# First 256 rows of k and q of batch 0 loaded in float32 by SyncE's queue, with the ALiBi table made in two parts

## The chip, the cores and the metric

The kernel runs on one core of a Trainium2 chip. The metric is the device time of one execution in microseconds (us), as the median over runs. The engines are TensorE (PE; its weight loads are PEld), VectorE (DVE), ScalarE (ACT), GpSimd (POOL) and SyncE (SP). DMAs are issued by an engine into its queue: POOL's is q0 in the profile, SP's is q1, and both are carried out by the core's 16 DMA engines.

## The reference

Sliding-window attention with ALiBi, then a feed-forward layer with ELU. All inputs and the output are float32.

```python
# q, k, v: (8, 8, 576, 64) = batch, heads, sequence, head size
scores = q @ k.T / 8 + slope[h] * -(abs(i - j))      # slope[h] = 2 ** -(h + 1)
scores = where((i >= j) & (i - j < 128), scores, -1e9)
attn = exp(scores - max) / (sum + 1e-9)
x = (attn @ v).transpose(0, 2, 1, 3).reshape(4608, 512)
h = x @ w_in                                          # (512, 2048)
out = where(h > 0, h, exp(min(h, 0)) - 1) @ w_out     # (2048, 512)
```

## The kernel before

Work is in float16 on TensorE with float32 sums in PSUM. Each batch of 576 rows goes through attention, is turned into columns of `xT`, and then feeds the two products of the feed-forward layer: `hidden` (L297, `x @ w_in`, matmuls at L305), `elu` (L319, DVE at L323) and `output` or the seven products of a Strassen scheme (L393). An order written out by hand interleaves these: steps ("slots") numbered from 0, with lists `early`, `HID`, `tasks`, `OUT` and `late` for each (L491 to L668). `at(s, f, ...)` puts a call into slot s. Each engine executes its instructions in the order in which they are written, and POOL also issues every load, in the order written, with at most eight loads of its queue unfinished at a time.

The change touches the opening, L428 to L488, which is ahead of slot 0. It goes through these stages:

- DVE fills `wz` with ones (L430) and TensorE runs 22 matmuls on it (`warm`, L465) that compute nothing that is used.
- POOL issues loads with `load_first` (L98), `load_v` (L112) and `load_wi` (L117), which round float32 to float16 on the way. First come rows 0 to 255 of k of batch 0 (L431), then the `iota` that the masks are made of (L432), the same rows of q (L433), two blocks of v (L434, L435), a quarter of `w_in` (L436), and the remaining rows of q and k. `split` (L90) says how the rows lie: rows 0 to 255 lie on 64 partitions with four rows each.
- DVE makes the identity, the bias row `RB` and `SI`, the identity scaled by each head's slope (L454 to L461). ScalarE makes the table `TAB[:, 0]` of exp(bias) for eight heads (L464).
- `turn_first` (L127) transposes q and k on TensorE into a PSUM bank and copies the bank into `K0` or `Q0`. It is called for each half of k (L466, L467; both copied by DVE) and of q (L469 by ScalarE, L470 by DVE). `early_bias` (L179) adds the bias to a bank by matmuls with `SI`.
- DVE copies `RB` (L471, L472) and `TAB` (L473, L474) into the shape of a batch's last unit. Batch 0 doesn't read `TAB`; batch 1 is the first that does (L216).
- `early_scores` (L186), `early_expo` (L194, ScalarE's exp) and `values` (L243, the product with v, then a division on DVE at L259 and L260) give the first 256 rows of attention. `turn` (L280) transposes them into `xT`, and the first `hidden` of slot 0 starts.

Slots 3 and 4 matter too. In slot 3 DVE's list holds `elu` of slot 2 (L323). In slot 4 it holds `values(0, 2, ...)`, that is a reciprocal (L259) and a product (L260) for each half, and then `elu` of slot 3. In slot 5 comes the copy of `turn(0, 2)` (L290).

`st` is a pair of buffers that hold q and k of batches 2 to 7 as loaded; the changed kernel borrows one of them once. `fore[2]` is a buffer that is first written in slot 13.

Of the kernel before, what the change touches and what calls it, by code (L numbers as in the profile page):

```python
# [7 lines left out]
F32 = mybir.dt.float32  # L8
F16 = mybir.dt.float16
I32 = mybir.dt.int32  # L10
AF = mybir.ActivationFunctionType
# [7 lines left out]
def kernel(  # L19
# [9 lines left out]
    nc = tc.nc  # L29
    B, H, S, D = q.shape  # L30
# [6 lines left out]
    R = S // 64  # L37
    V = nc.vector

    const = ctx.enter_context(tc.tile_pool(name="const", bufs=1))  # L40
    stage = ctx.enter_context(tc.tile_pool(name="stage", bufs=2))
# [7 lines left out]
    def one(shape, dt, name):  # L49
        return const.tile(shape, dt, name=name, tag=name)  # L50
# [6 lines left out]
    fore = [t.rearrange("p j c -> p (j c)") if t is not None else None for t in T]  # L57
    RB = fore[3][:, 1024:1536]
# [3 lines left out]
    TAB = one([128, 2, 4, 2, 256], F16, "TAB")  # L62
# [22 lines left out]
    st = {}  # L85
    s0 = gpool.tile([128, NFC * 512], F16, name="s0", tag="g")
    s1 = one([128, 2 * H * 6 * D], F16, "s1")
    s0 = [t[:, 0:2 * H * 6 * D].rearrange("p (w h j d) -> p w h j d", w=2, h=H, j=6) for t in (s0, s1)]

    def split(b, w, part):  # L90

        if b == 0 and w == 1:
            return ((0, 64, 4, 0, 0), (64, 64, 5, 256, 0))[part]
        if b == 0:
            return ((0, 64, 4, 0, 0), (64, 64, 2, 256, 0), (64, 64, 3, 384, 2))[part]
        return ((0, 128, 4, 0, 0), (0, 64, 1, 512, 4))[part]

    def load_first(b, w, part):  # L98

        p0, n, m, r0, j0 = split(b, w, part)  # L100
        nc.gpsimd.dma_start(
            s0[b][p0:p0 + n, w, :, j0:j0 + m, :].rearrange("p h j d -> p h (j d)"),
            (q, k)[w][b, :, r0:r0 + n * m, :].rearrange("h (p j) d -> p h (j d)", j=m))

    def load_qk(b, w, g):
        if b not in st:
            st[b] = stage.tile([128, 2, 2, R, 2, D], F16, name="st")
        nc.gpsimd.dma_start(  # L108
            st[b][32 * g:32 * g + 32, w, :, :, :, :].rearrange("p h n j d -> p (h n) (j d)"),
            (q, k)[w][b, 2 * g:2 * g + 2, :, :].rearrange("h (n i j) d -> i (h n) (j d)", i=32, j=2))  # L110

    def load_v(b, n):  # L112
        p = 128 if n < 4 else 64
        nc.gpsimd.dma_start(VP[b % 2][0:p, n, :, 0:D],  # L114
                            v[b, :, 128 * n:128 * n + p, :].rearrange("h p d -> p h d"))
# [11 lines left out]
    def turn_first(b, w, part, half, bank, copy):  # L127

        p0, n, m, r0, j0 = split(b, w, part)
        nh = 4 if n * m < 256 else 2  # L130
        t = bank.bitcast(F16)[:, 0:nh * m * n].rearrange("p (x j r) -> p x j r", x=nh, j=m)
        r = slice(p0, p0 + n)
        for x in range(nh):
            for j in range(m):
                for hh in range(2):
                    nc.tensor.transpose(t[64 * hh:64 * hh + 64, x, j, :], s0[b][r, w, 4 * hh + nh * half + x, j0 + j, :],
                                        ident[r, r])
        t = t.rearrange("p x j r -> p x r j")
        o = (Q0, K0)[w][b][:, nh * half:nh * half + nh, r0:r0 + m * n]
        copy(o.rearrange("p x (r j) -> p x r j", j=m), t)  # L140
# [8 lines left out]
    with tc.manual_schedule():  # L149
# [29 lines left out]
        def early_bias(banks, c0):  # L179

            for x in range(4):
                for hh in range(2):
                    nc.tensor.matmul(banks[hh][:, 128 * x:128 * x + 128], SI[:, 4 * hh + x, :], RB[:, c0:c0 + 128],
                                     start=x == 0, stop=False, skip_group_check=True)
# [58 lines left out]
        def values(b, i, part, bank=av):  # L243

            m = 128 if i < 4 else 64
            banks = (part, part + 2) if b < 2 else (2 * part, 2 * part + 1)
            parts = [(3, 128, 3), (3, 192, 4)] if i == 4 else [(i, 0, i)] + ([(i - 1, 128, i - 1)] if i else [])
            a = bank[:, 0:4 * (D + 1)].rearrange("p (x h d) -> p x h d", x=2, h=2)
            for x, g in enumerate(banks):
                for h2 in range(2):  # L250
                    for j, (u, c, n) in enumerate(parts):
                        c += 512 * g + 256 * h2
                        nc.tensor.matmul(a[:, x, h2, :], ex_[u][:, c:c + 128], VP[b % 2][:, n, 2 * g + h2, 0:D + 1],  # L253
                                         start=j == 0, stop=j == len(parts) - 1)
            if part == 0:
                xnt[b, i] = work.tile([128, 4, 2, D], F16, name="xn", tag="xn", bufs=4)
            o = xnt[b, i][0:m, part::2, :, :] if b < 2 else xnt[b, i][0:m, 2 * part:2 * part + 2, :, :]
            r = work.tile([128, 2, 2], F32, name="rden", tag="rden", bufs=2)
            V.reciprocal(out=r[0:m], in_=a[0:m, :, :, D])  # L259
            V.tensor_tensor(out=o, in0=a[0:m, :, :, 0:D], in1=r[0:m].unsqueeze(3).broadcast_to([m, 2, 2, D]),  # L260
                            op=ALU.mult)
# [18 lines left out]
        def turn(b, i, copy=None, bank=op):  # L280
            n = 128 if i < 4 else 64
            o = (b * S + 128 * i) % RING
            x = xnt.pop((b, i)).rearrange("p g h d -> p (g h d)")
            if copy is None:
                nc.sync.dma_start_transpose(out=xT[:, :, o:o + n], in_=x[0:n, :])
                return
            t = bank.bitcast(F16)[:, 0:512].rearrange("p (c r) -> p c r", c=4)
            for c in range(4):
                nc.tensor.transpose(t[:, c, 0:n], x[0:n, 128 * c:128 * c + 128], ident[0:n, 0:n])
            copy(xT[:, :, o:o + n], t[:, :, 0:n])  # L290
# [131 lines left out]
        def warm(n, bank=op):  # L422
            for _ in range(n):
                nc.tensor.matmul(bank[:, 0:256], wz[:, 0:128], wz, start=True, stop=True)
# [2 lines left out]

        rel = fore[3][:, 1536:2048].bitcast(I32)  # L428
        far = fore[1][:, 0:256]
        V.memset(wz, 1.0)  # L430
        load_first(0, 1, 0)  # L431
        nc.gpsimd.iota(rel, pattern=[[1, 256]], base=0, channel_multiplier=-1)  # L432
        load_first(0, 0, 0)  # L433
        load_v(0, 0)  # L434
        load_v(0, 1)  # L435
        load_wi(0)  # L436
        load_first(0, 0, 1)
        load_first(0, 1, 1)
        load_first(0, 0, 2)
# [16 lines left out]
        V.tensor_scalar(out=far, in0=far, scalar1=0.0, scalar2=-BIG, op0=ALU.is_gt, op1=ALU.mult)  # L456
        V.scalar_tensor_tensor(out=RB[:, 0:256], in0=rel, scalar=-1.0, in1=far, op0=ALU.mult, op1=ALU.add)
        slope = [2.0 ** (-8.0 * (h + 1) / H) for h in range(H)]
        for h in range(H):
            V.tensor_scalar(out=SI[:, h, :], in0=ident, scalar1=8.0 * slope[h], scalar2=None, op0=ALU.mult)  # L460
        V.memset(VP[0][:, :, :, D:D + 1], 1.0)  # L461

        for h in range(H):
            nc.scalar.activation(TAB[:, 0, h // 2, h % 2, :], RB[:, 0:256], AF.Exp, scale=slope[h])  # L464
        warm(22)  # L465
        turn_first(0, 1, 0, 0, hp[0], V.tensor_copy)  # L466
        turn_first(0, 1, 0, 1, op, V.tensor_copy)  # L467
        early_bias(AB, 0)
        turn_first(0, 0, 0, 0, hp[1], nc.scalar.copy)  # L469
        turn_first(0, 0, 0, 1, av, V.tensor_copy)  # L470
        V.tensor_copy(RB[:, 256:448], RB[:, 0:192])  # L471
        V.tensor_copy(RB[:, 448:512], RB[:, 0:64])  # L472
        V.tensor_copy(TAB[:, 1, :, :, 0:192], TAB[:, 0, :, :, 0:192])  # L473
        V.tensor_copy(TAB[:, 1, :, :, 192:256], TAB[:, 0, :, :, 0:64])  # L474
        early_bias(sp[2:4], 128)
        early_scores(AB, 0, 0)
        early_expo(AB, 0, 0)
# [6 lines left out]
        values(0, 0, 1, op)  # L484
        warm(5, sp[0])
        turn(0, 0, V.tensor_copy, hp[0])
        values(0, 1, 0)
        values(0, 1, 1, op)  # L488

# [3 lines left out]
        def at(s, f, *a):  # L493
            tasks.setdefault(s, []).append((f, a))
# [7 lines left out]
        def before(s, f, *a):  # L502
            early.setdefault(s, []).append((f, a))
# [20 lines left out]
        for o in range(16 * NTB):  # L524
            t, ts, f = o // 16, o // 4 % 4, o % 4
# [8 lines left out]


        at(0, turn, 0, 1, V.tensor_copy)
        at(0, turn_first, 0, 0, 1, 0, sp[3], nc.scalar.copy)
        before(1, done, 0)
        at(1, early_bias, AB, 128)
# [59 lines left out]
        for b in range(2, B):  # L599
            for u in range(4):  # L600
                a = START[b] + 4 * u
# [11 lines left out]
            a = START[b - 1] if b > 2 else 0  # L613
# [85 lines left out]
```

The softmax here doesn't subtract the row's maximum and nothing guards it: scores larger than these inputs give would overflow.

## Time and profile before

| what | value |
|---|---|
| median of 3 runs | 310.82 us (310.35 to 310.94) |
| span of the profiled execution, first to last instruction | 308.9 us |
| share of the span in which PE is busy | 97% |
| DVE, ACT, POOL | 83%, 78%, 35% |
| mean rate of the DMA engines | 104 GB/s, 32.04 MB |
| bytes of POOL's queue q0, of SP's queue q1 | 18.36 MB, 12.98 MB |
| mean granted TensorE clock | 0.998 |

The profile is of one execution. It gives a span and no separate time for that execution; the median lies 1.9 us above the span, which is what passes ahead of the first and after the last instruction. The bytes of a transfer are counted as written, so a load that rounds float32 to float16 reads twice what is shown.

The profile has a page with busy times, a strip of 40 time slices, the chain of work that ended last and the costliest groups of instructions. The trace behind it can be asked for the instructions of a stretch in order of time, for the waits of an engine, for the chain in a stretch, and for the packets of each DMA queue in a stretch.

### The profile page before, as it was taken

The numbers are of one execution on the slowest core, as the hardware profiler recorded it, in microseconds if no ns is written. First come the engines' busy times: TensorE is split into PE (matmuls) and PEld (weight loads), VectorE is DVE, ScalarE is ACT, GpSimd is POOL, SyncE is SP. The second block draws the span as 40 slices with busy tenths as digits, with TensorE's granted clock in tenths as the row PEclk, the third lists the DMA queues.
The fourth block names the chain that finished last, engine by engine and source line by source line (L and its number), as shares of the span: only waits on it lengthen the run. The fifth ranks groups of instructions, "written<-read, shape, count | busy, mean of one in ns | idle before, by whom it ended". The sixth has DMA issues, their size and how long they took to land.

```text
span 308.9 us, 9820 instructions
## 1 busy us (share of the span) xinstructions
PE 300.1 (97%) x4071; PEld 256.1 (83%) x4071; DVE 257.5 (83%) x498; ACT 241.8 (78%) x446; POOL 108.4 (35%) x163
## 2 busy tenths in 40 slices
PE   6899999999999999999999999999999999999995
PEld 4788875798888888988888888888899888898884
DVE  4646888988989998997989998989998788886782
ACT  4576678678798788878887889778888897968871
POOL 8937867273252315141616061706000001010000
PEclk9999999999999999999999999999999999999999
DMA  9999999999194919395969896999530202030103
GB/s 96 196 197 202 201 180 185 94 118 115 21 165 63 169 35 161 43 152 59 132 70 138 110 102 78 138 124 122 60 94 7 91 17 87 19 98 0 70 28 110
DMA packets 96509, 32.04 MB, mean 104 GB/s; under 512 B 83920, under 2 KB 91984, under 8 KB 96464
## 3 DMA queue, kind: packets, MB, share of 16 engines
q0 software_dynamic: 75920, 18.36, 64.2%
q1 hardware_dynamic: 20400, 12.98, 17.1%
q8 instruction: 32, 0.52, 0.7%
q14 instruction: 13, 0.11, 0.1%
q10 hardware_dynamic: 144, 0.07, 0.1%
HBM read 36.70 MB, written 9.44 MB: 149 GB/s over the span
## 4 chain that ended last, share of the span: by engine, by line
PE 72%; DVE 8%; DMA 6%; ACT 5%; POOL 4%; issue 4%; POOLq 0%; DVEq 0%
PE hp L305 33%; PE op L393 13%; PE av L393 12%; DMA VP<-in_v_dram 4%; PE spa L225 3%; PE spa L271 3%; DVE g L323 3%; POOL e L316 2%; PE sp L393 2%; ACT e L315 2%; DMA s<-in_q_dram 2%; ACT EX L236 1%; PE sp L253 1%; POOL VP L114 1%; DVE xn L260 1%
## 5 line engine op out<-in xcount | busy, mean ns | idle before, releaser
L305 PE MATMUL hp<-xT,wi 128*128 128x256 f16 (+3 forms) x1488 | 144.2, 245 | 1.0 <-DVE g L323 0.5
L305 PEld LDWEIGHTS <-wi 128*128 128x128 f16 x1600 | 119.9, 98 | 18.1 <-issue 6.3
L323 DVE SCALAR_TENSOR_TENSOR g<-e,hp 128x512 f16<-128x512 f32 x138 | 93.7, 679 | 22.2 <-ACT e L313 12.5
L316 POOL TENSOR_SCALAR e<-e 128x512 f32<-128x512 f32 x44 | 28.0, 636 | 158.8 <-ACT e L315 152.9
L312 ACT ACTIVATE e<-hp 128x512 f32<-128x512 f32 x98 | 58.6, 597 | 28.5 <-PE hp L305 23.1
L313 ACT ACTIVATE e<-e 128x512 f32<-128x512 f32 x100 | 63.1, 631 | 3.2
L393 PEld LDWEIGHTS <-S 128*128 128x128 f16 x544 | 51.2, 98 | 6.7 <-issue 0.6
L393 PEld LDWEIGHTS <-g 128*128 128x128 f16 x408 | 38.2, 98 | 4.7 <-issue 0.6
L241 DVE TENSOR_TENSOR EX<-EX,TAB 128x1024 f16<-128x1024 f16 x48 | 32.9, 686 | 6.2 <-ACT EX L236 4.0
L114 POOL DMA_DIRECT2D VP<-in_v_dram x40 | 34.6, 878 | 0.6 <-PE hp L305 0.3
L315 ACT ACTIVATE e<-hp 128x512 f32<-128x512 f32 x40 | 24.1, 601 | 10.9 <-PE hp L305 10.9
L393 PE MATMUL op<-T,S 128*128 128x256 f16 x200 | 30.0, 273 | 0.1
L233 ACT ACTIVATE EX<-spa 128x1024 f16<-128x1024 f32 x24 | 24.6, 1025 | 3.7 <-PE spa L225 3.4
L393 PE MATMUL av<-T,S 128*128 128x256 f16 x176 | 26.4, 273 | 0.1
L236 ACT ACTIVATE EX<-sp 128x512 f16<-128x512 f32 x48 | 26.0, 596 | 0.0
L354 DVE TENSOR_TENSOR S<-g 128x1024 f16<-128x1024 f16 (+2 forms) x35 | 23.5, 671 | 0.8 <-PE op L393 0.2
L393 PE MATMUL op<-wo,g 128*128 128x256 f16 x128 | 19.2, 272 | 0.1
L393 PE MATMUL av<-wo,g 128*128 128x256 f16 x120 | 18.0, 272 | 0.0
L277 DVE TENSOR_TENSOR xn<-spa,rden 128x512 f16<-128x512 f32 x24 | 16.6, 692 | 0.8
L108 POOL DMA_DIRECT2D st<-in_k_dram x24 | 16.2, 686 | 2.8 <-DMA s<-in_q_dram 1.9
L108 POOL DMA_DIRECT2D st<-in_q_dram x24 | 15.9, 666 | 0.6 <-DMA VP<-in_v_dram 0.6
L271 PE MATMUL spa<-VP,EX 128*128 128x65 f16 x336 | 15.4, 193 | 0.1
(139 smaller groups left out, 379.3 us busy)
## 6 DMA issues: line engine op xcount, KB each, us to landing
out_dram<-ob SPq DMA_DIRECT2D x35, 256.0 KB, 2.2
VP<-in_v_dram POOLq DMA_DIRECT2D x32, 128.0 KB, 5.7
st<-in_k_dram POOLq DMA_DIRECT2D x24, 144.0 KB, 5.2
st<-in_q_dram POOLq DMA_DIRECT2D x24, 144.0 KB, 5.9
wi<-in_moe_w_in_dram POOLq DMA_DIRECT2D x4, 512.0 KB, 10.7
wo<-in_moe_w_out_dram POOLq DMA_DIRECT2D x4, 512.0 KB, 10.1
VP<-in_v_dram POOLq DMA_DIRECT2D x8, 64.0 KB, 5.8
s<-in_k_dram POOLq DMA_DIRECT2D x1, 512.0 KB, 12.1
```

What stands on the lines that cost most here:

```text
L108: nc.gpsimd.dma_start(st[b][32 * g:32 * g + 32, w, :, :, :, :].rearrange("p h n j d -> p (h n) (j d)"), (q, k)[w][b, 2 * g:2 * g + 2, :, : ...
L114: nc.gpsimd.dma_start(VP[b % 2][0:p, n, :, 0:D], v[b, :, 128 * n:128 * n + p, :].rearrange("h p d -> p h d"))
L236: nc.scalar.activation(unit(b, u)[:, g, :, :], sp[g].rearrange("p (h c) -> p h c", h=2), AF.Exp, scale=0.125)
L241: V.tensor_tensor(out=e, in0=e, in1=TAB[:, int(u == 3), 2 * gp:2 * gp + 2, :, :], op=ALU.mult)
L271: nc.tensor.matmul(a[:, h // 4, h % 4, :], ex_[u][:, c:c + 128], VP[b % 2][:, n, h, 0:D + 1], start=j == 0, stop=j == len(parts) - 1)
L305: nc.tensor.matmul(p[:, l * w + u0:l * w + u1], w_in_sb[:, c, fc * 128:(fc + 1) * 128], xT[:, c, x0:x0 + u1 - u0], start=(c == 0), stop=(c ...
L312: nc.scalar.activation(e[:, 0:n], p[:, 0:n], AF.Relu, scale=-1.0)
L313: nc.scalar.activation(e[:, 0:n], e[:, 0:n], AF.Exp, scale=-1.0)
L315: nc.scalar.activation(e[:, 0:n], p[:, 0:n], AF.Exp)
L316: nc.gpsimd.tensor_scalar(out=e[:, 0:n], in0=e[:, 0:n], scalar1=1.0, scalar2=0.0, op0=ALU.min, op1=ALU.max)
L323: V.scalar_tensor_tensor(out=gs[t][:, f0:f0 + nf, c0:c0 + w], in0=sh(es.pop((t, c0, f0))), scalar=1.0, in1=sh(hps.pop((t, c0, f0))), op0=A ...
L393: nc.tensor.matmul(o, a[:, j, :], b[:, j, :], start=j == 0 and i in (1, 2, 5), stop=j == 7, skip_group_check=True)
```

## The change

The 256-row loads of k and q of batch 0 leave POOL's queue. SP issues them instead, ahead of everything else in its queue, without rounding: `load_raw` puts float32 into one of the `st` buffers, on 128 partitions with two rows each. `cook` rounds them into `fore[2]`, k by DVE and q by ScalarE, each in two halves. `turn_first` reads `fore[2]` for these rows, with 8 transposes of 128 partitions for each half where there were 16 of 64.

The matmuls of `warm` ahead of this are 14 instead of 22. The table `TAB[:, 0]` is made for four heads at its old place and for the other four after `turn(0, 0)`. The two copies into `TAB[:, 1]` move from the opening to slot 3, where they are written after `elu` of slot 2.

```diff
     def split(b, w, part):
 
         if b == 0 and w == 1:
-            return ((0, 64, 4, 0, 0), (64, 64, 5, 256, 0))[part]
+            return ((0, 128, 2, 0, 0), (64, 64, 5, 256, 0))[part]
         if b == 0:
-            return ((0, 64, 4, 0, 0), (64, 64, 2, 256, 0), (64, 64, 3, 384, 2))[part]
+            return ((0, 128, 2, 0, 0), (64, 64, 2, 256, 0), (64, 64, 3, 384, 2))[part]
...
+    raw = stage.tile([128, 2, 2, R, 2, D], F16, name="st")
+    raw = raw.rearrange("p a b n j d -> p (a b n j d)").bitcast(F32)[:, 0:2048].rearrange(
+        "p (w h j d) -> p w h j d", w=2, h=H, j=2)
+    cooked = fore[2].rearrange("p (w h j d) -> p w h j d", w=2, h=H, j=2)
+
+    def load_raw(w):
+
+        nc.sync.dma_start(raw[:, w, :, :, :].rearrange("p h j d -> p h (j d)"),
+                          (q, k)[w][0, :, 0:256, :].rearrange("h (p j) d -> p h (j d)", j=2))
+
+    def cook(w, half, copy):
+
+        o, i = [t[:, w].rearrange("p (a b x) j d -> p b a (x j d)", a=2, b=2)[:, half] for t in (cooked, raw)]
+        copy(o, i)
...
+        src = cooked if b == 0 and part == 0 else s0[b]
...
-                    nc.tensor.transpose(t[64 * hh:64 * hh + 64, x, j, :], s0[b][r, w, 4 * hh + nh * half + x, j0 + j, :],
+                    nc.tensor.transpose(t[64 * hh:64 * hh + 64, x, j, :], src[r, w, 4 * hh + nh * half + x, j0 + j, :],
                                         ident[r, r])
...
+        load_raw(1)
+        load_raw(0)
         V.memset(wz, 1.0)
-        load_first(0, 1, 0)
         nc.gpsimd.iota(rel, pattern=[[1, 256]], base=0, channel_multiplier=-1)
-        load_first(0, 0, 0)
         load_v(0, 0)
...
+        def table(h0, h1):
+            for h in range(h0, h1):
+                nc.scalar.activation(TAB[:, 0, h // 2, h % 2, :], RB[:, 0:256], AF.Exp, scale=slope[h])
...
-        for h in range(H):
-            nc.scalar.activation(TAB[:, 0, h // 2, h % 2, :], RB[:, 0:256], AF.Exp, scale=slope[h])
-        warm(22)
+        table(0, 4)
+        warm(14)
+        for half in range(2):
+            cook(1, half, V.tensor_copy)
+        for half in range(2):
+            cook(0, half, nc.scalar.copy)
         turn_first(0, 1, 0, 0, hp[0], V.tensor_copy)
...
-        V.tensor_copy(TAB[:, 1, :, :, 0:192], TAB[:, 0, :, :, 0:192])
-        V.tensor_copy(TAB[:, 1, :, :, 192:256], TAB[:, 0, :, :, 0:64])
...
         turn(0, 0, V.tensor_copy, hp[0])
+        table(4, H)
...
         at(0, turn, 0, 1, V.tensor_copy)
+        at(3, V.tensor_copy, TAB[:, 1, :, :, 0:192], TAB[:, 0, :, :, 0:192])
+        at(3, V.tensor_copy, TAB[:, 1, :, :, 192:256], TAB[:, 0, :, :, 0:64])
```

## The prediction, made blind

> **What bounds the kernel now.** I read the page's busy times and strip first, then PE's waits, then the chain of the first 36 us, then the instructions there in order of time.
>
> ```profile
> PE 300.1 (97%) x4071; PEld 256.1 (83%) x4071; DVE 257.5 (83%) x498; ACT 241.8 (78%) x446; POOL 108.4 (35%) x163
> PE   6899999999999999999999999999999999999995
> DMA  9999999999194919395969896999530202030103
> ```
>
> TensorE is the bound: 97% busy, and outside the first slice and the last it hardly pauses. So time taken out of the opening comes off the end, if nothing after it gives it back. The DMA strip warns of what might: the DMA engines are full from the first slice to about 55 us. PE's waits in the first 60 us (total, times, longest) show what the opening waits for:
>
> ```profile
> PE op L424 <- DVE T L430: 1.2, 1, 1.2
> PE hp L136 <- DMA s<-in_q_dram: 1.0, 1, 1.0
> ```
>
> The second is q's load. The chain (start, length, what) says the same:
>
> ```profile
> 2.47 5.16 DMA s<-in_q_dram
> 7.63 0.04 issue
> 7.68 0.44 PE hp L136 x16
> ```
>
> The load of q, issued at 2.47, lands at 7.63, and the rest waits for it; k landed at 5.46 (its issue at 1.25 plus 4.2). From there to the first exp:
>
> ```profile
> 8.16 0.58 ACT L140 COPY QT<-hp 128x512 f16<-128x512 f16 x1 [1.70 <-PE hp L136]
> 8.41 0.69 DVE L140 COPY QT<-av 128x512 f16<-128x512 f16 x1 [1.18 <-PE av L136]
> 8.85 0.59 PE L191 MATMUL spa<-QT,KT 64*128 64x128 f16 x8
> 9.48 1.02 ACT L197 ACTIVATE EX<-spa 128x1024 f16<-128x1024 f32 x1 [0.74 <-PE spa L191]
> ```
>
> The exp starts at 9.48, which is 1.85 us after q. I measure the front of the change at this exp.
>
> **When q lands after the change.** SP is released with the others: ACT's first instruction is at 0.74, so I put both issues at about 0.75. The trace has no load on SP's queue. The nearest row for its start is a store on it: issued at 64.92 beside little other traffic, its packets began about 0.85 us later (17 in the first microsecond, then 127 in the next). So first packets at about 1.6. q0's first, rounded load of k was slow for 1.2 us (147 packets from 2.7 to 3.9) and then ran at 380 packets a microsecond, each reading 1024 bytes: 389 GB/s. The new packets are 512 bytes, 1024 of them for each tensor, so the same rate is 760 a microsecond. POOL's first v load now comes about 1.5 us earlier, issued at 1.65, since two issues of 0.84 and 0.71 us are gone; with the 1.35 us that k took from issue to packets its traffic starts at 3.0. Until then SP's queue is alone: 1.4 us times 760 is 1060 packets, so k is through and lands at about 3.6 (k's old lag from last packet to landing was 0.6). Then q shares with v. Packet for packet, a pair moves 512 + 256 bytes, at 389 GB/s 506 pairs a microsecond, so q's 1024 packets take 2.0 us: last at 5.0, landing at **5.6**. That is the estimate I take, because k's old load is the row closest in tensor, direction and engines.
>
> The other end: how does q1 fare beside a busy q0? A store was issued at 40.71 while q0 was deep. In the window 43.7 to 44.7 us (packets, MB, share of time):
>
> ```profile
> q0 software_dynamic: 735, 0.09, 202.3%
> q1 hardware_dynamic: 54, 0.11, 40.5%
> ```
>
> Its first packets came 3.0 us after issue, and it landed after 5.9 us where quiet stores took 2.1. Transposes on q1, with small packets, ran at 250 a microsecond beside 387 of q0 (88.8 to 89.8) and at 276 almost alone. If 276 is what q1 can do with small packets from the start, q is last at 1.6 + 2048/276 = 9.0 and lands at 9.5. So the landing lies between 4.9 (no sharing at all, 1.6 + 2.7 + 0.6) and 9.5.
>
> The Trainium skill speaks against this part: DMA: Bandwidth & Descriptors, Rules for kernel authors, says that spreading DMAs over SP, ACT and GpSimd gives no bandwidth, since all run on the same 16 engines and interleave, and saves issue time only. The 43.7 window agrees that they interleave. By the rule alone q would gain only its earlier start; the no-gain rival below is about that.
>
> **From q's landing to the exp.** Two roundings on ScalarE come in between. A 128x512 float32 pass in SBUF is 0.63 us (L313); the second follows a pitch of about 0.53 later (the table's eight of 256 take 2.56, so 0.32 each, plus half of the 0.42 that separates 1024 from 512 elements). Both are done at landing + 0.05 + 0.53 + 0.63 = 1.21. TensorE's 8 transposes of the second half: 16 of this form run at a pitch of 0.47 with a tail of 0.17 (batch 1's at 42.62), so 0.41, against 0.42 for the old 16. Then DVE's copy 0.69, the last scores and the tail 0.38 as before (9.10 to 9.48), and 0.06 of gaps: 1.21 + 0.41 + 0.69 + 0.38 + 0.06 = 2.75, which is 0.90 more than 1.85. With q at 5.6 the exp starts at 8.35, **1.13 earlier**. Without any other effect the break-even landing is 6.73.
>
> k's two roundings on DVE cost nothing while q is last. The trace has no such form; the bounds are 0.40 (the copy at L472) and 0.69 (L140) each, and up to 0.7 more where a copy waits for a POOL issue (below). k would then be in `K0` at the latest by 3.6 + 2.8 + 0.45 + 0.69 = 7.5, and the scores need it at 8.0. The cover is 0.5 us; without it the exp moves with k.
>
> **Warm-up.** The first 14 or 15 of the 22 `warm` matmuls run at a pitch of 0.21 us and the others at 0.107, so the clock doubles at about 4.2. The 14 that remain end there too, and k's transposes follow within a microsecond; a gap of 1.0 us (6.7 to 7.7) did not slow TensorE before. I take nothing. If it stayed at half pitch, about 0.5 us of matmuls ahead of the exp and the 0.9 us of each `hidden` would double for a while: 0.5 to 1.5 us lost.
>
> **The table.** Four activations less ahead of q: ScalarE is done at about 4.3 instead of 6.46, so it is free for q. The four that move cost 4 x 0.32 = 1.28, and lie between the exp that ends at 12.46 and the one at 14.10, in an idle stretch of 1.63. Nothing, with 0.35 to spare. The waiting roundings at the head of ScalarE and DVE hold up only the turns, which need the same data.
>
> **The copies into TAB[:, 1]** leave a place where DVE had slack (idle 0.39 at 10.90) and come after this line:
>
> ```profile
> 22.20 0.69 DVE L323 SCALAR_TENSOR_TENSOR g<-e,av 128x512 f16<-128x512 f32 x1 [2.44 <-POOL e L316]
> 23.77 0.18 DVE L259 RECIPROCAL rden<-av 128x4 f32<-128x4 f32 x1 [0.88 <-PE av L253]
> ```
>
> There are 0.88 us between them. DVE is then busy without a break until 27.1, and the chain runs along it (rden, xn, g, xT, g, then ACT, POOL, g, and PE at 29.23 after waiting 0.32). What exceeds 0.88 is lost. The price from this trace:
>
> ```profile
> 9.02 0.50 DVE L471 COPY T<-T 128x192 f16<-128x192 f16 x1
> 9.22 0.72 DVE L473 COPY TAB<-TAB 128x1536 f16<-128x1536 f16 x1
> 9.86 0.65 DVE L474 COPY TAB<-TAB 128x512 f16<-128x512 f16 x1
> ```
>
> Both took 9.22 to 10.51, 1.29 us: a loss of 0.41. But the size doesn't explain these: 192 elements took 0.50, 1536 took 0.72, 512 took 0.65, and the first and last ended 0.10 and 0.08 after a DMA issue on POOL did (9.42 and 10.43). Without the delay, 0.40 + 0.2 would fit into 0.88 and cost nothing. POOL is as busy at 22.9 (DMA issues at 22.12 and 23.59, e at 23.03), so I take 0.3, nearer to the row.
>
> The Trainium skill explains it: SBUF — State Buffer, Who interferes with whom, says that a VectorE copy in a two-port mode and GpSimd exclude each other for a whole instruction. These rows agree. By it the loss here is nearer 0.4 than 0, and k's roundings meet POOL's back-to-back issues.
>
> **Loads behind.** All bytes read stay the same, and the stream starts about 1 us earlier, so w_in's first quarter, which landed at 11.86 (5.16 + 6.7), comes at about 11. The first `hidden` would want it at 13.01 - 1.13 = 11.9. Were it not earlier, the gain would still be 1.1. Later loads have 1.5 us or more (w_in's third quarter lands at 20.9 and is used at 22.42).
>
> **Sum.** 308.9 - 1.13 + 0.3 = 308.1 of span, and the same shift from the median: 310.82 - 0.83 = **310.0**. On the chip 0.2% is 0.62 us, about what a measurement of this kernel can tell from no change.
>
> **Rivals.** *No change:* q shares more evenly and lands at 6.0 to 6.9; the exp gains 0.7 or loses 0.2, and the copies take 0.3: 310.7. For it: q0 and q1 interleave in every window that has both; against: SP has the first 1.4 us to itself. *Slower:* q1 with small packets gets about 267 a microsecond beside q0, as the transposes did. From 3.0 q needs 3.8 us and lands at 7.4; the exp is at 10.2, 0.7 late, plus 0.3: **311.9**, and 313.8 if 276 holds from the start. It decides from a landing of 6.5 on (9.48 - 2.75 - 0.3 = 6.43). Against: the rounded loads ran at 380 to 1200 packets a microsecond. That the loads don't move to SP's queue is excluded: they carry no wait and stand first there.
>
> **Chances.** Faster as forecast 0.45, no change 0.25, slower 0.30. The range runs from 308.8 (q at 4.9 and no loss at the copies: 310.82 - 1.83 = 309.0, a little less if later waits shrink) to 312.9, short of the far end of the slow case. The forecast's own range is 309.2 to 310.2.
>
> **What would show it.** Right: q's two packet phases over by 5.0, the first exp near 8.35, `hidden` near 11.9, DVE's rden in slot 4 up to 0.4 later against its neighbours, and a span near 308.1. Wrong: q landing after 6.5, a q1 rate near 270, k's roundings stretched past 2.8 us, matmuls at 0.21 pitch after 5 us, or a new PE wait on w_in.

## The result, and the profile after

The changed kernel takes 311.73 us (median of 15 executions, 310.96 to 312.17), against 310.79 (309.85 to 311.43) for the kernel before in the same comparison. The ratio is 1.0028 [1.0018, 1.0038]: slower by 0.9 us, where a gain of 0.8 was forecast. The profiled execution has a span of 310.4 us against 308.9. Of the 15 executions 8 ran at a mean granted clock of 0.994 to 0.995 and took 311.72 to 312.17 us; 7 ran at 0.999 or 1.0 and took 310.96 to 311.73, four of them 311.43 or more. The profiled execution is one of the 8.

The page has it in its strip. These are TensorE's busy time, its strip and that of the granted clock:

```profile
PE 300.9 (97%) x4031; PEld 256.1 (83%) x4031; DVE 258.9 (83%) x500; ACT 243.0 (78%) x448; POOL 106.8 (34%) x161
PE   5999999999999999999999999999999999999995
PEclk9799999999999999999999999999999999999999
```

TensorE is busy 0.8 us longer than before although it runs 40 matmuls less, and the second slice (7.8 to 15.5 us) has a 7 in the clock's row. The kernel before had 9 everywhere. PE's waits in the first 60 us (total, times, longest):

```profile
PE hp L152 <- DVE T L118: 1.4, 1, 1.4
PE op L440 <- DVE T L448: 1.2, 1, 1.2
PE hp L152 <- ACT T L118: 0.6, 1, 0.6
```

The wait of 1.0 for q's load has become two: 1.4 us for k's rounding on DVE and 0.6 for q's on ScalarE. The chain (start, length, what) shows what set the end:

```profile
0.74 0.46 SPq L112
1.26 5.70 DMA st<-in_q_dram
6.99 1.15 ACT T L118 x2
8.18 0.64 PE av L152 x6
```

q was issued 1.2 us earlier than before, but took 5.70 instead of 5.16, so it landed at 6.96, only 0.67 earlier. From there to the exp and the first `hidden`, in order of time:

```profile
7.66 0.41 PE L152 MATMUL hp<-ident,T 128*64 128x128 f16 x8 [0.64 <-ACT T L118]
8.11 0.59 ACT L156 COPY QT<-hp 128x512 f16<-128x512 f16 x1
8.18 0.64 PE L152 MATMUL av<-ident,T 128*64 128x128 f16 x8
8.86 0.69 DVE L156 COPY QT<-av 128x512 f16<-128x512 f16 x1 [1.39 <-PE av L152]
9.71 0.61 PE L207 MATMUL spa<-QT,KT 64*128 64x128 f16 x8
10.36 1.02 ACT L213 ACTIVATE EX<-spa 128x1024 f16<-128x1024 f32 x1 [1.66 <-PE spa L207]
14.41 1.05 PE L321 MATMUL hp<-xT,wi 128*128 128x128 f16 x16
```

The eight transposes at 8.18 take 0.64 where eight of the same form took 0.41 at 7.66. The exp starts at 10.36, 0.88 later than before. The first `hidden` starts at 14.41 instead of 13.01, which is 1.40 later: the other 0.5 is lost between the two, where the clock is low until 11.6. After slot 4 (`hidden` at 30.59, before 29.23) it is 1.36, and the span ends 1.5 later.

### The profile page after: what moved, and what is told of

Its sections match the earlier page's. It is cut to its first block, busy times and chain, and to the rows that moved or that the text cites. A ratio compares the mean times of both kernels' runs of the same rounds, so it can differ in the third digit from the quotient of the medians.

```text
span 310.4 us, 9747 instructions
## 1 busy us (share of the span) xinstructions
PE 300.9 (97%) x4031; PEld 256.1 (83%) x4031; DVE 258.9 (83%) x500; ACT 243.0 (78%) x448; POOL 106.8 (34%) x161
## 4 chain that ended last, share of the span: by engine, by line
PE 71%; DVE 8%; ACT 6%; DMA 6%; POOL 4%; issue 4%; SPq 0%; POOLq 0%; DVEq 0%; ACTq 0%
PE hp L321 32%; PE av L409 12%; PE op L409 12%; DMA VP<-in_v_dram 4%; PE spa L241 3%; PE spa L287 3%; DVE g L339 3%; POOL e L332 2%; ACT e L331 2%; DMA st<-in_q_dram 2%; PE sp L409 2%; ACT EX L252 2%; POOL VP L129 1%; PE sp L269 1%; DVE S L370 1%
```

## The experiments

Two theories stood after this. *A*: the warm-up of 14 matmuls leaves TensorE idle for too long, and the granted clock falls. *Rival* (theory B in the expectations): q's late landing and the roundings make up the loss by themselves. The expectations use letters for these and for smaller questions (the copies, the table, the start of a queue), and say what each holds. Each kernel was timed beside the kernel before on the same chip. `w22`, `loads_only`, `tables_only` and `hybrid` were timed together (before: 310.63), `w14_before`, `w22_at2`, `hybrid2` and `early_small` together (310.90), and `hybrid2_again`, `hybrid2_w14` and `tables_at2` together (310.57); `w14_bias` was timed by itself (310.88). Between these groups it is the ratios to the kernel before that can be compared. With each median stands the range of its executions.

**The warm-up alone (two runs).** The first, `w22`, is the changed kernel with 22 matmuls:

```diff
-        warm(14)
+        warm(22)
```

> The changed kernel with 22 warming matmuls ahead of k's transposes, as before the change, in place of 14; all else as changed. In the changed kernel's profile TensorE idled from 4.36 to 5.72 and the granted clock was 0.50 from 8.1 to 11.6. Theory A (the shorter warm-up lets the clock fall in part of the executions): the clock is 1.0 throughout, the first exp comes 2.75 after q's landing (9.7 if q lands at 6.96) where the changed kernel had 3.40, and the median falls by 0.4 to 0.5 to about 311.3. Theory B (only the late landing of q and the two roundings cost): the clock doesn't depend on the warm-up, the median stays at 311.7.

310.98 us (310.83 to 311.12), ratio 1.0011 [1.0001, 1.0021]. All 12 executions ran at 0.999 or more. More than half of the loss is gone; the two intervals of the ratio barely overlap, and all 12 executions lie below 13 of the changed kernel's 15. The windows of both kernels (us, then busy time and instructions of each engine, granted clock, time of the DMA packets as a share of the 16 engines' time, GB/s; 1.72 is 172%), the changed kernel first, then the one with 22:

```profile
4.00:8.10 4.10, 2.07 (x34) 1.21 (x32) 2.26 (x7) 1.35 (x3) 3.77 (x6) 1.00 1.72 232
8.10:11.60 3.50, 3.42 (x40) 2.71 (x40) 0.99 (x3) 1.84 (x4) 3.28 (x11) 0.51 1.38 198
```

```profile
4.00:8.10 4.10, 3.42 (x44) 2.26 (x42) 2.27 (x7) 1.43 (x4) 3.87 (x7) 1.00 1.72 232
8.10:11.60 3.50, 3.48 (x61) 2.52 (x61) 1.51 (x6) 2.50 (x5) 3.29 (x11) 1.00 1.38 198
```

The loads and DVE's roundings are the same in both, or nearly so (DMA share and DVE of the first stretch). TensorE is busy for 2.07 us of the first 4.1 in one and 3.42 in the other, and afterwards the clock is 0.51 in one and 1.00 in the other. With 22 matmuls the exp and the first `hidden` start here:

```profile
9.62 1.02 ACT L213 ACTIVATE EX<-spa 128x1024 f16<-128x1024 f32 x1 [1.00 <-PE spa L207]
13.14 1.05 PE L321 MATMUL hp<-xT,wi 128*128 128x128 f16 x16
```

ScalarE began on q at 6.90, so the exp comes 2.72 later.

> The kernel before with 14 warming matmuls in place of 22, nothing else. TensorE then idles from about 4.3 until k lands (5.4 to 5.6) and again until q lands. Theory A (the pause after a short warm-up lets the granted clock fall to 0.50 for a few us in part of the executions): mean granted clocks of 0.994 to 0.995 appear in a good part of the executions, and the median rises by 0.3 to 0.7 to 311.0 to 311.3. Rival (the clock fell in the changed kernel for another reason, such as its later exp): no executions below 0.998, time as before, 310.6.

`w14_before`, the kernel before with `warm(14)` instead of `warm(22)`: 312.54 us (310.97 to 314.76), ratio 1.0050 [1.0027, 1.0073]. So fewer matmuls hurt without any of the new loads. The profiled execution had the clock at 0.50 from 7.9 to 14.7. But this run supports A by half only: 6 of the 12 executions ran at 0.998 or more, and these took 312.17 to 313.19, no less than the others. And q landed at 8.3 in its profile, 0.7 later than before, with the issue at the same time. Part of its 0.5% has another cause, which stays open.

**The parts of the change (three runs).** First, as `loads_only`, the loads without the table: whole table and copies at their old places, 22 matmuls.

```diff
-        table(0, 4)
-        warm(14)
+        table(0, H)
+        warm(22)
...
+        V.tensor_copy(TAB[:, 1, :, :, 0:192], TAB[:, 0, :, :, 0:192])
+        V.tensor_copy(TAB[:, 1, :, :, 192:256], TAB[:, 0, :, :, 0:64])
...
-        table(4, H)
...
-        at(3, V.tensor_copy, TAB[:, 1, :, :, 0:192], TAB[:, 0, :, :, 0:192])
-        at(3, V.tensor_copy, TAB[:, 1, :, :, 192:256], TAB[:, 0, :, :, 0:64])
```

> The changed loads and roundings alone: 22 warming matmuls, the whole table in its old place, the copies into TAB[:, 1] in the opening. Theory B (q lands at about 7.0 and two roundings come behind it): exp at about 9.7 where the kernel before had 9.48, time 0.2 to 0.3 above the kernel before, about 311.1. Theory A alone (all loss from clock): equal to the kernel before, 310.8. Theory C alone: also 310.8. If the whole table in front held up q's rounding, the rounding would start after q's landing by more than 0.1; the table should end near 5.5, so not.

310.85 us (310.66 to 311.02), ratio 1.0007 [0.9997, 1.0018], exp at 9.65. The new loads of k and q bring nothing: the exp comes 0.17 later than before. Then, as `tables_only`, the table without the loads (the kernel before, with the table split and the copies in slot 3):

> The kernel before with the table made in two parts and the two copies into TAB[:, 1] moved to slot 3; loads and warm-up as before. Theory C (the moved copies delay DVE's chain in slots 4 and 5): the reciprocal of slot 4 starts 0.1 to 0.4 later against its neighbours and the time is 0.1 to 0.4 above the kernel before, 310.9 to 311.2. Rival: they fit into DVE's pause of 0.88 and the time is that of the kernel before, 310.8.

310.62 us (310.09 to 312.85), ratio 1.0014 [0.9997, 1.0032]: no difference can be told. From the start of the last `g` ahead of `rden` to `rden` itself it is 1.70 us (22.10 to 23.80), against 1.57 before. In this execution q happened to land at 7.15 and the exp to start at 8.99, 0.49 earlier than before; the first `hidden` followed at 12.72, 0.29 earlier, and the second at 15.06, 0.11 earlier. Of the 0.49, 0.20 went ahead of the first `hidden`, where TensorE's weight load waited 0.17 for w_in, and 0.18 at the second line of PE's waits:

```profile
PE op L424 <- DVE T L430: 1.2, 1, 1.2
PE sp L136 <- DMA s<-in_q_dram: 0.5, 1, 0.5
PE hp L136 <- DMA s<-in_q_dram: 0.3, 1, 0.3
```

`sp` is the turn of q's rows 256 to 383, whose load then lands last. Last, as `w22_at2`, `w22` with the copies in slot 2 instead of 3, where DVE had a pause:

> The changed kernel with 22 warming matmuls, and the copies into TAB[:, 1] written into slot 2, so that they stand ahead of elu of slot 2 on VectorE and not behind it. There VectorE pauses for 2.4 us. Theory C (the copies cost 0.12 at slot 3, by the distance of g to the reciprocal: 1.70 with them, 1.57 without): that distance goes back to 1.57 and the time falls by about 0.1 from the 22-matmul kernel's 310.98 to 310.85. Rival: the later DVE work absorbs it and the time is the same.

310.80 us (310.66 to 311.06), ratio 0.9990 [0.9973, 1.0007]. DVE's rows, of the changed kernel first and of this one second, show what became of the copies:

```profile
23.44 0.69 DVE L339 SCALAR_TENSOR_TENSOR g<-e,av 128x512 f16<-128x512 f32 x1 [2.44 <-POOL e L332]
24.04 1.17 DVE L688 COPY TAB<-TAB 128x1536 f16<-128x1536 f16 x2
25.14 0.17 DVE L275 RECIPROCAL rden<-av 128x4 f32<-128x4 f32 x1
```

```profile
22.51 0.69 DVE L339 SCALAR_TENSOR_TENSOR g<-e,av 128x512 f16<-128x512 f32 x1 [1.77 <-POOL e L332]
24.08 0.18 DVE L275 RECIPROCAL rden<-av 128x4 f32<-128x4 f32 x1 [0.88 <-PE av L269]
```

From `g` to `rden` it is 1.70 in the first and 1.57 in the second, as before the change. At this place the copies in slot 3 cost 0.13 us, and those in slot 2 nothing.

**What the load of q can be worth (two runs).** In the first, `hybrid`, only q goes through SP in float32, so nothing is ahead of it there. k is POOL's first load, behind the `iota`, and lies and is rounded as before. q is rounded by DVE and turned first. 22 matmuls. Its edit of the changed kernel, without `split` and `src`:

```diff
-        load_raw(1)
         load_raw(0)
         V.memset(wz, 1.0)
...
+        load_first(0, 1, 0)
...
-        warm(14)
-        for half in range(2):
-            cook(1, half, V.tensor_copy)
-        for half in range(2):
-            cook(0, half, nc.scalar.copy)
-        turn_first(0, 1, 0, 0, hp[0], V.tensor_copy)
-        turn_first(0, 1, 0, 1, op, V.tensor_copy)
-        early_bias(AB, 0)
+        warm(22)
+        cook(0, 0, V.tensor_copy)
+        cook(0, 1, V.tensor_copy)
         turn_first(0, 0, 0, 0, hp[1], nc.scalar.copy)
         turn_first(0, 0, 0, 1, av, V.tensor_copy)
+        early_bias(AB, 0)
+        turn_first(0, 1, 0, 0, hp[0], nc.scalar.copy)
+        turn_first(0, 1, 0, 1, op, V.tensor_copy)
```

> Only q goes through SyncE's queue in float32 and is rounded by VectorE; k stays rounded on GpSimd's queue, now first there; q is turned ahead of k; 22 warming matmuls; tables as in the changed kernel. If SyncE's queue has the DMA engines to itself until it is drained, as in the changed kernel's packets (q0 silent until 5.4), q's 1024 packets are over at about 4.2 and land at 4.7, and k's 512 follow at 380 a microsecond to 5.6 and land at about 6.2: first exp at about 8.4 to 8.6, time about 1 below the kernel before, 309.8. Rival: a queue's first packets are slow for 1.2 us wherever they start, so k lands at 7 or later and the exp comes at 9.2 or later: 310.5 to 311.

310.47 us (309.99 to 311.19), ratio 0.9996 [0.9983, 1.0009]. The expected gain didn't come. q's packets were over by 4.5, but it landed at 5.6 and not at 4.7; k, whose packets began at 3.6 beside q's, landed at 6.9, and the exp started at 9.43, near what the rival had. The second run, `hybrid2`, puts the bias matmuls ahead of the turns and the copies into slot 2:

> As the hybrid (q alone through SyncE's queue in float32, rounded by VectorE; k rounded on GpSimd's queue), with the first bias matmuls moved ahead of the turns, where TensorE idles, and the copies into TAB[:, 1] in slot 2. In the hybrid's profile k landed at 6.94 but was turned only from 7.62, behind q's turn and the bias. Expected: k turned from about 7.1, exp at 8.9 to 9.0 (0.5 earlier than the kernel before's 9.48), time 0.4 to 0.6 below the hybrid's 310.47, about 310.0. Rival (later loads are the next bound: in the tables-only kernel the exp came at 8.99 and the second hidden still waited 0.5 for q's rows 256 to 383): no gain past the first hidden, 310.4.

310.27 us (309.78 to 310.94), ratio 0.9979 [0.9967, 0.9992]: faster than the kernel before by 0.2%, though not by as much as expected. The exp starts at 9.26 and not at 9.0, the first `hidden` at 12.85.

**The start of a queue.** `early_small` is the kernel before, with a load of 64 KB on SP ahead of all others, whose data is not used:

> The kernel before, and SyncE issues a load of 64 KB in float32 (128 pieces of 512 bytes, of q, not used) ahead of everything, at about 0.74. In the two kernels the first 1.1 to 1.2 us of packets were slow, on whichever queue came first (q0: 2.7 to 3.9, q1: 1.8 to 2.9). Theory D (the slow start belongs to the DMA engines' first packets of the program): the small load takes it from 1.8 to 2.9, k's packets run at full rate from their start near 2.7 to 2.9, k and q land 0.8 to 1.0 earlier (4.5 and 6.7), and the exp comes near 8.6; time up to 0.5 below the kernel before, less where later loads bound. Theory E (each queue has its own slow start, or the start depends on GpSimd's descriptors): q0's slow phase stays, q lands at about 7.6, time as before.

310.95 us (309.94 to 312.02), ratio 0.9999 [0.9985, 1.0013]. Nearly all of SP's packets, 129 of 144, came between 1.8 and 2.1. POOL's first load was slow nevertheless: 36, 51, 11 and 55 packets in the four stretches of 0.3 us from 2.7, and 113 in the next. So what is slow at the start isn't the first packets of the DMA engines, whoever sends them. What it is stays open.

**Where the gain of the combined version comes from, and the warm-up again (four runs).** `hybrid2_again` repeats `hybrid2`, the combined version, as a partner; `hybrid2_w14` is the same with `warm(14)`; `tables_at2` is `tables_only` with the copies in slot 2; `w14_bias` is the changed kernel with the bias matmuls moved up:

```diff
         warm(14)
+        early_bias(AB, 0)
...
-        early_bias(AB, 0)
```

> The same kernel as before under the name hybrid2, run a second time as the partner of the two others on the same chip. If its gain is real, the ratio to the kernel before is again 0.997 to 0.999, with no execution at a mean granted clock below 0.997.

310.19 us (309.76 to 310.55), ratio 0.9984 [0.9973, 0.9994], no execution under 0.998: the gain holds.

> The kernel before with the table made in two parts and the two copies in slot 2 instead of slot 3, all loads as before. If the gain of the combined version comes from q's earlier load, this one agrees with the kernel before within 0.2% and lies 0.4 to 0.9 us above the combined version. Rival (the gain comes from the copies' new place and the free stretch that they leave on DVE in the opening): this one is as fast as the combined version, 0.15 to 0.3% below the kernel before. The distance from the gelu input g of slot 2 to rden is 1.57, as in the version with the copies in slot 2 of the changed kernel.

310.30 us (310.03 to 312.81), ratio 0.9996 [0.9977, 1.0015]; from `g` to `rden` (`g` is a result of `elu`, which the expectation calls gelu) it is 1.57. It lies 0.11 above the combined version where 0.4 to 0.9 was expected, so how much of that version's gain is due to q's load and how much to the table isn't settled.

> The combined version with 14 warm-up matmuls instead of 22 and nothing else changed. Theory A (the shorter warm-up lets the granted clock fall, whenever TensorE waits between it and the first turns): the profile or several of the executions show a mean clock of 0.988 to 0.996, and the median is 0.5 to 1.5 us above that of the version with 22. Rival (the fall needs the late q of the changed kernel, with a wait of TensorE around 7.0): here q comes first and lands about 5.5, so the clock stays at 0.998 or more and the two medians agree within 0.3 us.

309.87 us (309.58 to 311.42), ratio 0.9985 [0.9967, 1.0002]; one execution of 12 ran at 0.994, the others at 0.998 or more, though two of these took 310.70 and 311.42. Here 14 matmuls do no harm that can be told; in the profiles they even help, since the 22 and the bias end at 6.84, after q was rounded, and hold up its turn (6.78 against 5.71). So the number of matmuls alone doesn't decide.

> The changed kernel with its 14 warm-up matmuls, and with the 8 bias matmuls of the first bank moved ahead of k's turn, where TensorE waited 1.36 us; nothing else is changed. Theory A in the form that the last runs suggest (not the number of warm-up matmuls counts, but TensorE's idle time between them and the scores): no wait over 0.8 us is left ahead of k's turn, the executions stay at a mean granted clock of 0.998 or more, the profiled exp starts near 9.6 as with 22 matmuls, and the ratio to the kernel before is 0.9995 to 1.0015, near that of the version with 22. Rival (the count of matmuls in the warm-up itself decides, 14 against 22): the granted clock falls to 0.50 in about half of the executions as in the changed kernel, and the ratio is 1.0025 or more. A second rival (the wait between k's turn and q's decides, which becomes longer here, about 1.1 us, as the bias no longer stands there): also a fall, but from about 8.5 on and not ahead of it.

311.73 us (310.96 to 312.19), ratio 1.0023 [1.0009, 1.0038]. Eight of the 12 executions ran at 0.993 to 0.995 and took 311.63 to 312.19; four ran at 1.0 and took 310.96 to 311.09. The gap between the groups, some 0.9 us, is the price of the fall in this kernel. My expectation failed: the matmuls moved up filled the wait ahead of k's turn, but opened one ahead of q's. PE's waits of this kernel, and then of `hybrid2_w14`, to the scores:

```profile
PE hp L152 <- ACT T L118: 1.0, 1, 1.0
PE hp L152 <- DVE T L118: 0.5, 1, 0.5
```

```profile
PE hp L152 <- DMA s<-in_k_dram: 0.5, 1, 0.5
PE hp L152 <- DVE T L118: 0.5, 1, 0.5
```

Neither the count of matmuls nor the longest wait orders the kernels; what goes with the falls is the sum of TensorE's waits between warm-up and scores. In the profiles it is 0.6 with no fall in 12 executions (`w22`), 1.05 with one in 12 (`hybrid2_w14`), 1.1 with one in 12 (`early_small`), 1.2 with 8 in 116 (before, beside the experiments), 1.3 with none in 12 (`w22_at2`), 1.5 with 8 in 12 (`w14_bias`), 2.0 with 8 in 15 (the changed kernel), and 2.8 with 6 in 12 (`w14_before`); a fall is counted where the mean clock is under 0.997. The order is not proof: one profile stands for all executions of a kernel, and where q comes through POOL its landing varies. `tables_only` has 0.3 in its profile and two falls in 12, `tables_at2` 0.65 and one; `loads_only`, `hybrid`, `hybrid2` and its repeat have 0.4 or less and none.

## Why the prediction was wrong

**The warm-up** is the step that failed: "I take nothing". It had the price right in kind (half pitch for a while) and dismissed it because a gap of 1.0 us had done no harm before and k's turn was to follow within a microsecond. But k landed at about 5.0 and not at 3.6, so the changed kernel has waits of 1.36 and 0.64 us, and in about half of its executions the clock then falls. In the profiled one the exp loses 0.65 to it (10.36 against 9.62 + 0.09 for ScalarE's later start), and up to the first `hidden` 1.2 us are lost (14.41 against 13.14 and the same 0.09). Over all executions the change of 14 to 22 is worth 0.0017 of the ratio, 0.5 us. The fall that the mean clock shows isn't all of it: of the changed kernel's 7 executions without it only three (310.96 to 311.13) are as fast as those of `w22`. What slowed the other four, no trace shows. The cover that I should have priced is the clock's own: how long TensorE may do little before the clock is taken away.

The two profiled falls tell something of how. TensorE's busy time ahead of the fall, in the low stretch, and up to its end, of `w14_before`:

```profile
4.50:7.90 3.40, 1.24 (x40) 1.03 (x40) 1.56 (x5) 1.95 (x7) 3.40 (x5) 1.00 1.83 168
7.90:11.30 3.40, 2.93 (x56) 2.48 (x57) 1.83 (x5) 0.90 (x2) 3.35 (x5) 0.51 1.21 150
11.30:14.70 3.40, 3.40 (x35) 2.50 (x34) 1.27 (x5) 2.70 (x5) 3.23 (x11) 0.50 1.47 190
```

and in the same way of the changed kernel and of the kernel before:

```profile
4.80:8.20 3.40, 1.74 (x34) 1.23 (x34) 2.18 (x4) 1.22 (x3) 3.06 (x5) 1.00 1.83 211
8.20:11.60 3.40, 3.40 (x40) 2.68 (x40) 0.99 (x3) 1.74 (x3) 3.19 (x11) 0.50 1.38 198
```

```profile
4.80:8.20 3.40, 2.17 (x76) 1.67 (x74) 1.36 (x3) 1.70 (x7) 3.40 (x6) 1.00 1.90 170
```

The last is of `w14_bias`, whose profiled execution had no fall:

```profile
4.80:8.20 3.40, 1.78 (x36) 1.19 (x34) 2.32 (x4) 1.39 (x3) 3.25 (x5) 1.00 1.83 208
```

The low stretches last one and two times 3.4 us. The clock fell after 3.4 us in which TensorE was busy for 1.24 and 1.74, stayed with 1.78 and 2.17, didn't come back after 2.93 and came back after 3.40. Between 1.74 and 1.78 no threshold can be read, and `w14_bias`, with 1.78 in its profile, fell in 8 of its 12 executions: the busy time of a stretch doesn't decide alone. The Trainium skill, TensorE: Matmul & The Clock Gate, Part 1, has a free-running window of about 3.4 us, half rate after an idle window and full rate after a busy one. The length agrees with these traces; that the window runs freely would explain why only some executions fall. The idleness that it asks for doesn't agree: in these windows TensorE was busy for 36 and 51% of the time. That a window decides is a reading of these rows, and where it begins was read from the falls; no run placed the work against it on purpose.

**q's landing** was mis-sized: forecast 5.6, measured 6.96, past the break-even of 6.73. The packets of the changed kernel show where the 1.36 us went, in the windows 1.8 to 2.8, 3 to 4, and 5.7 to 6.0 us (packets, MB, share of time):

```profile
q1 hardware_dynamic: 131, 0.07, 24.1%
```

```profile
q1 hardware_dynamic: 677, 0.35, 114.4%
```

```profile
q1 hardware_dynamic: 134, 0.07, 93.5%
q0 software_dynamic: 84, 0.01, 55.9%
```

I had 760 packets a microsecond from 1.6 on, so 1060 by 3.0. The queue began at 1.8 and was slow until 2.9, as q0's first load had been: 210 by 3.0. Those 850 packets at the rate of the second window, 677, are 1.26 us. I had written down that slow start for q0 and not given it to q1. The rate was 11% below mine in the second window and 25% below (some 570) from 4.5 to 5.4. The lag from the last packet (6.2) to the landing was near 0.8 instead of 0.6. That is more than 1.36, because another term went the other way: I let q share packet for packet with v from 3.0, and v's load, issued at 1.35, sent nothing until 5.4, when q had some 340 packets left. The rule of the Trainium skill that I weighed (DMA: Bandwidth & Descriptors, Rules for kernel authors: no bandwidth from spreading) agrees with this: 677 packets of 512 bytes a microsecond are 347 GB/s, less than q0's 389 by itself. Its interleaving shows from 5.4 on and not before.

**From the landing to the exp** I had 2.75. With the clock at full speed it is 2.74 (`w22`, landing at 6.88); in the changed kernel it was 3.40. The step was right, and its condition didn't hold. With the landing at 6.96 it puts the exp at 9.71, 0.23 late; `w22` has 0.14 and `loads_only` 0.17, as q landed slightly earlier there.

**The copies** cost 0.13 and not 0.3: the two took 1.17 us there, against 1.29 in the opening. **The table** in two parts cost nothing, as forecast: its second half takes 1.36 us in ScalarE's pause. **k's roundings** on DVE took 0.89, inside the bounds. w_in's first quarter landed at 10.86 (forecast 11), and nothing waited for it.

**The rivals.** The time, 311.73, is near that of the slower one (311.9), whose condition, a landing after 6.5, came true. Its mechanism didn't: q1 ran at 570 to 690 packets a microsecond, not at 267. That the time came near is luck: 0.5 us of the loss is the warm-up's. With 22 matmuls the change costs a ratio of 1.0011; in the profile the exp is 0.14 late and the copies add 0.13, about the 0.3 by which its span is longer (309.2 against 308.9).

**The premise** that time taken out of the opening comes off the end held for the losses. For a gain it held only in part in the profile of `tables_only`, where an exp 0.49 earlier left 0.11 at the second `hidden`; in that of `hybrid2_w14` an exp 0.67 earlier (8.81) went with a span 0.8 shorter.

Two slips of the prediction changed nothing: its DMA strip is full for ten slices, to 77 us and not 55, and the far end of the landing, 9.0 and a lag of 0.6, is 9.6.

## What to carry to other kernels

A warm-up is not dead weight that ends where the real work begins: before it is shortened, add up what TensorE will be busy for in the few microseconds after it, and look at the granted clock of many executions, since one profile may show either case. A load moved to an idle queue still pays that queue's start and shares the same engines, so count its packets from the trace of the queue's first load, not from its steady rate. And a load that lands earlier can move the wait to the next one: in `tables_only` w_in and the later rows of q took back most of what an earlier exp had gained.

## What the runs showed of the hardware

- A queue's first large load is slow for about 1.1 us on either queue: q1 sent 131 packets from 1.8 to 2.8 (177 in `w22`) and then 677 a microsecond; q0 sent 147 from 2.7 to 3.9 and then 380. A small load ahead on the other queue doesn't change that for q0.
- While q1 had a backlog, q0 sent nothing for 2 to 3 us, though its load had been issued at 1.35; in `hybrid` q0 began at 3.6. In both, q1 then had 320 to 340 packets left.
- The pitch of the warm-up matmuls, 0.21 us, is half speed, but the clock's row of the page has 9 there. So a mean clock of 1.0 doesn't show how late the clock first rose. In the profiles it rose between about 4.0 (`w22_at2`) and 6.8 (`hybrid2_again`). That may be why `w14_before`, and four executions of the changed kernel, were slow at a mean clock of 1.0 too; no trace of such an execution was taken.
- The rounding load of q through POOL, issued at the same time in each kernel, landed between 7.15 and 8.3 us in the profiles of `tables_only`, `tables_at2`, the kernel before and `w14_before`. The float32 load of q behind k on SP landed within 0.2 us of 6.9 in each, and these kernels' executions with 22 matmuls lie within 0.4 us of each other; those of the kernel before lie 1.6 to 3.3 us apart.
